# FFT, MLP and soft mixture of experts in one kernel: the float64 conversion's temporaries move to PSUM, w_out @ phi is summed the other way round, the tail's loads wait for the last split, and the order of all instructions is made anew

## The chip, the cores and the metric

One NeuronCore of a Trainium2 chip runs the whole program. The metric is the device time of one execution in microseconds (us), lower is better. The time before is the median of three runs. Engines are named as the profile names them: PE (TensorE, matrix products), PEld (its weight loads), DVE (VectorE), ACT (ScalarE), POOL (GpSimd) and SP (SyncE, which only issues DMAs here).

## What is computed

Three stages run one after the other on 8 sequences of 3072 rows and 256 columns: the real part of a two-dimensional DFT, an MLP whose activation is h - tanh(h), and a soft mixture of 8 experts with 4 slots each.

```python
X = np.fft.fft(np.fft.fft(x, axis=1), axis=2).real.astype(np.float32)   # x: 8 x 3072 x 256
x = X.reshape(8 * 3072, 256)
h = x @ w_in                                # w_in: 256 x 2048
x = ((h - np.tanh(h)) @ w_out).astype(np.float32)
logits = x @ phi                            # phi: 256 x 32
d = softmax of logits over all 24576 rows   # dispatch
slot_out[e] = np.maximum((d.T @ x)[e] @ w1[e], 0) @ w2[e]
c = softmax of logits over the 32 slots     # combine
out = c @ slot_out
```

`w_in` and `w_out` are float64 in memory and reach the chip as pairs of 32-bit words. The chip has to turn them into float32 itself.

## The kernel before

**Three stages.** The *head* loads `w_in` and `w_out` in 16 units of 128x512 numbers (4 chunks `c`, each with two units of either matrix), converts each to float32, and makes the weights of the main loop from them: `Wh`/`Wl` (`w_in` times a small DFT matrix, as a high and a low part), the transposes `winT` and `woT`, products for the logits (`h_1`), and `wp` = `w_out @ phi`. In the same time the 24-point part of the FFT of the first sequence is done in SBUF by POOL, DVE and ACT (`dft24`, line 327 for the additions and 331 for the scalings). The *main loop* runs over 96 tiles of 128 frequency rows, each with 4 groups `g` of 512 hidden columns. The *tail* computes the experts' MLP for the 32 slots and then mixes and stores 8 sequences.

**The conversion** (`load_w`, lines 770 to 814). A unit arrives in `raw`, low and high words alternating. ACT squares the high word read as float32 (`square`, L784) into `cv`. DVE then does six operations of 128x512: `top` (L787, a TENSOR_SCALAR), `sign` (L790), `small` (L794), `power` (L798, a TENSOR_SCALAR), `low` (L802) and `join` (L805). All inputs and outputs are in SBUF: `raw`, `cv`, and the result in `tr`. `cv` has two buffers, so two units are in work at a time.

**w_out @ phi.** Per chunk, `wo_t` (L832) turns `w_out` into `woT`, `wp_t` (L841) multiplies with `phi` as the stationary operand into 32 rows of 512, ACT copies that into a corner of the second sequence's buffer (`wpT`, L962), and after the last chunk `wp_1` (L929) turns it back with 16 transposes.

**A group of the main loop.** PE makes two products `pp` and `qq` (`wide`, L462). DVE moves `pp` to SBUF with a correction (`evac`, L483) and forms `h` (`plus`, L488), POOL the mirror half (`minus`, L491), ACT takes tanh (`act_h`, L500) and rounds to float16 (`act_t`, L508), DVE forms the rest (`low_t`, L512, "t1" below), SP issues a transposing DMA (`turn_t`, L516, into `tt`), and PE adds the result to the logits (`logits`, L543). Two tiles form a pair `p`: its logits give softmax factors, and `slots` (L650) adds to the slots' sums.

**The order.** Each engine runs its instructions in the order in which the program issues them. That order is made when the program is built: a class `Flow` simulates the engines with a cost per operation, rings of buffers (`"B": 7` are the PSUM banks, `"cv"`, `"t"`, `"tt"` and others) and due times from the table `SCHED`, and always issues the operation that can start first. `+B` in an operation's list of buffers asks that one more bank stays free when it takes its own. One Flow plans the head, one the main loop with the tail's first loads, one the tail.

**The tail's loads.** `early` are ten loads into buffers that the main loop has done with (`wot`, `wlw`, `w128w`); they wait until the last group's products are evacuated. `late` are 16 loads of `w2`, 512 KB each, into slots of `tr`. The first `EARLY` = 2 of them are planned in the main loop's Flow, the others in the tail's, behind three loads of saved logits (`load_l`, `lt`).

Of the kernel before, what the change touches and what calls it, by code (L numbers as in the profile page):

```python
# [9 lines left out]
F32 = mybir.dt.float32  # L10
# [38 lines left out]
    "wide0": -0.16, "wide1": 0.762, "z_dft": -4.233, "ls_sum": 13.766, "soft_m": 15.943, "soft_h": 16.77,
    "soft_l": 17.545, "z_acc": 28.408, "evac": 1.257, "z_high": -3.8, "z_low": -1.921, "z_copy": -1.709,  # L50
    "z_turned": 0.891, "low_t0": 4.415, "low_t1": 4.601, "plus": 2.019, "minus": 2.76, "soft_e": 15.988,
    "ls_keep": 14.024, "act_h0": 2.352, "act_h1": 4.079, "act_t0": 4.217, "act_t1": 4.386, "acc_add": 34.456,
    "soft_x": 13.986,
# [172 lines left out]
def fft_mlp_softmoe_kernel(ctx: ExitStack, tc: tile.TileContext, x, w_in, w_out, phi, w1, w2, cq, fd, cm, ct, out):  # L226
# [536 lines left out]
    def clear(_):
        nv.memset(spec, 0.0)
        nv.memset(zacc, 0.0)
        nv.memset(zts[:, :, 0:1], 1.0)
        nv.memset(spt[:, 0:1], 1.0)
        nv.memset(nm[0], 3.0e38)

    def load_w(dst, src, a, u):  # L770
# [37 lines left out]
        hf.add({"A": ca(512)}, square, [("raw", u)], [("f", u)], take="cv")
        hf.add({"V": 0.34}, top, [("raw", u)], [("v", u)])
        hf.add({"V": 0.6}, sign, [("raw", u)], [("v", u)])  # L810
        hf.add({"V": 0.6}, small, [("f", u)], [("v", u)])
        hf.add({"V": 0.34}, power, [("v", u)], [("f", u)])
        hf.add({"V": 0.6}, low, [("raw", u)], [("f", u)], free="raw")
        hf.add({"V": cv(512), "G": cg_(512)}, join, [("v", u), ("f", u)], [u], free="cv")
# [4 lines left out]

    def psum(key, a=None, n=512, rows=128):  # L820
        t = bank(str(key).replace(" ", ""), "hps", n, rows)
        Y[key] = t if a is None else t.rearrange("p (a b) -> p a b", a=a)
        return Y[key]

    def B(*key):
        return f"B:{key}".replace(" ", "")
# [787 lines left out]
```

## Time and profile before

| what | value |
|---|---|
| median of 3 runs | 1541.09 us (1539.62 to 1548.11) |
| the profiled execution: its own time | 1543.61 us |
| its span, first to last instruction | 1541.8 us |
| mean granted TensorE clock | 0.969 of full speed |
| PE busy | 1422.7 us (92% of the span) |
| DVE busy | 1200.6 us (78%) |
| ACT busy | 1147.2 us (74%) |
| POOL busy | 1022.6 us (66%) |

Busy time is summed over the whole span. Shares over the span mix the three stages, whose limits differ, so a stage is read from its own window. "Idle before, releaser" in a row of the trace says how long the engine stood still before the instructions, and what ended it.

### The profile page before, as it was taken

To read this page: it belongs to the slowest core of one execution; us is meant where nothing else is said; L and a number is where in the kernel's file an instruction comes from. 1 tells how busy PE (TensorE), PEld (TensorE's weight loads), DVE (VectorE), ACT (ScalarE), POOL (GpSimd) and SP (SyncE) were. 2 spreads that over 40 slices of the span, in tenths; PEclk is the share of its full clock that TensorE was granted. 3 is DMA by queue.
4 is the path that set the end of the run, shared out by engine and by line. 5 is a ranking of instruction groups with operands and counts; after the bars stand their busy time and mean duration, and the time that the engine had idled before them with its cause. 6 is when DMAs were issued, how large, how long until landed. Compare 5 with 4: busy or idle time off the path is not lost. (4 is left out here: it accounts for less than half of the span.)

```text
span 1541.8 us, 37758 instructions
## 1 busy us (share of the span) xinstructions
PE 1422.7 (92%) x14604; PEld 1053.2 (68%) x14604; DVE 1200.6 (78%) x2046; ACT 1147.2 (74%) x2527; POOL 1022.6 (66%) x760
## 2 busy tenths in 40 slices
PE   2769999999999999999999999999999999996786
PEld 1337777777677777777677777777777767764464
DVE  8998788878788888878787888888787778774462
ACT  2337887878788878888788788887888777773386
POOL 3965589867886897579857986788678922321320
PEclk9789999999999999999999999999999999997899
DMA  6328999989999999999989999999999999889978
GB/s 192 122 74 180 196 198 196 179 152 192 179 180 162 201 183 193 170 191 196 185 150 194 186 190 164 187 201 189 166 182 185 194 178 191 153 169 240 306 291 363
DMA packets 856867, 292.87 MB, mean 190 GB/s; under 512 B 803440, under 2 KB 847344, under 8 KB 854896
## 3 DMA queue, kind: packets, MB, share of 16 engines
q1 hardware_dynamic: 856688, 290.47, 95.4%
q8 instruction: 114, 1.87, 0.5%
q14 instruction: 65, 0.53, 0.1%
HBM read 58.15 MB, written 30.67 MB: 58 GB/s over the span
## 5 line engine op out<-in xcount | busy, mean ns | idle before, releaser
L491 POOL TENSOR_TENSOR h<-pb,h 128x512 f32<-128x512 f32 x288 | 369.1, 1286 | 302.5 <-DVE h L488 270.5
L512 DVE SCALAR_TENSOR_TENSOR tr<-th,tr 128x512 f16<-128x512 f32 x576 | 387.9, 685 | 38.8 <-ACT tr L508 36.5
L500 ACT ACTIVATE th<-h 128x512 f32<-128x512 f32 x576 | 339.9, 602 | 72.8 <-DVE h L488 36.8
L462 PE MATMUL pp<-Wh,zh 128*128 128x512 f32 x960 | 377.2, 410 | 0.2
L462 PE MATMUL qq<-Wh,zh 128*128 128x512 f32 x768 | 333.0, 434 | 5.4 <-DVE pb L483 3.3
L508 ACT ACTIVATE tr<-th 128x512 f16<-128x512 f32 x576 | 332.5, 596 | 7.2 <-ACT qq L497 2.1
L483 DVE SCALAR_TENSOR_TENSOR pb<-W,zts,pp 128x512 f32<-128x512 f32 x288 | 214.7, 746 | 109.1 <-PE pp L462 92.6
L543 PEld LDWEIGHTS <-tt 128*128 128x128 f16 x6144 | 194.9, 96 | 77.5 <-issue 42.6
L543 PE MATMUL L<-WPn,tt 128*128 128x64 f16 (+1 forms) x6144 | 226.2, 185 | 23.3 <-DMA tt<-tr 22.9
L488 DVE SCALAR_TENSOR_TENSOR h<-pb,qq 128x512 f32<-128x512 f32 x288 | 196.2, 684 | 50.4 <-PE qq L462 42.6
L462 PEld LDWEIGHTS pp<-Wh,zh 128*128 128x128 f32 x960 | 182.0, 190 | 44.2 <-issue 1.6
L462 PE MATMUL pp<-Wl,zh 128*128 128x512 f32 x480 | 190.8, 397 | 0.0
L462 PEld LDWEIGHTS qq<-Wh,zh 128*128 128x128 f32 x768 | 146.7, 191 | 51.1 <-DVE tr L512 9.9
L327 POOL TENSOR_TENSOR xb<-xb 128x508 f32<-128x508 f32 (+3 forms) x98 | 150.5, 1541 | 22.0 <-DMA xb<-in_x 14.1
L462 PE MATMUL qq<-Wl,zh 128*128 128x512 f32 x384 | 152.1, 396 | 0.0
L650 PE MATMUL ta<-tr,dh 128*32 128x512 f16 x2304 | 145.6, 389 | 0.0
L327 POOL TENSOR_TENSOR tA<-xb 128x1024 f32<-128x1024 f32 (+2 forms) x69 | 107.0, 1559 | 23.7 <-ACT xb L331 20.7
L462 PEld LDWEIGHTS pp<-Wl,zh 128*128 128x128 f32 x480 | 91.3, 190 | 15.1
L650 PEld LDWEIGHTS <-dh 128*32 128x32 f16 x2304 | 56.1, 98 | 61.2 <-issue 12.5
L327 POOL TENSOR_TENSOR xb<-xb,tA 128x512 f32<-128x512 f32 (+1 forms) x46 | 78.2, 1699 | 19.6 <-DVE xb L327 16.1
L327 POOL TENSOR_TENSOR xb<-tA 128x508 f32<-128x508 f32 (+2 forms) x78 | 84.9, 1095 | 1.6 <-DVE tA L327 1.2
L454 ACT COPY zts<-tps 128x256 f32<-128x256 f32 x96 | 35.7, 372 | 67.3 <-PE tps L450 66.7
(263 smaller groups left out, 2485.1 us busy)
## 6 DMA issues: line engine op xcount, KB each, us to landing
out<-xb SPq DMA_DIRECT2D x14, 1536.0 KB, 5.4
xb<-in_x SPq DMA_DIRECT2D x32, 512.0 KB, 5.0
tr<-in_moe_w SPq DMA_DIRECT2D x16, 512.0 KB, 9.1
tt<-tr SPq DMA_TRANSPOSE x385, 4.8
xb<-in_moe_w SPq DMA_DIRECT2D x12, 512.0 KB, 4.3
raw<-in_moe_w_in SPq DMA_DIRECT2D x8, 512.0 KB, 3.7
xb<-in_x SPq DMA_DIRECT2D x16, 256.0 KB, 3.9
...
```

The lines of the kernel that those rows point to most:

```text
L327: fn = lambda e: e.tensor_tensor(out=out[1](), in0=a[1](), in1=c[1](), op=op)
L454: ns.copy(out=zs[i][3][:, 1:257], in_=zpp.pop(i).rearrange("p a b -> p (a b)"))
L462: nt.matmul(o, z, v, start=first and n == 0, stop=last and n == 2)
L483: nv.scalar_tensor_tensor(out=pb, in0=W128[:, c - (c > FOLD), :], scalar=zs[i][3][:, 129:130], in1=pqs.pop((g, 0)), op0=ALU.mult, op1=ALU.add)
L488: nv.scalar_tensor_tensor(out=hs[g][:, 0, :], in0=pbs[g], scalar=0.5, in1=pqs.pop((g, 1)), op0=ALU.mult, op1=ALU.add)
L491: ng.tensor_tensor(out=hs[g][:, 1, :], in0=pbs.pop(g), in1=hs[g][:, 0, :], op=ALU.subtract)
L500: ns.activation(out=o, in_=hs[g][:, k, :], func=AF.Tanh)
L508: ns.activation(out=place_t(g)[:, 0, k], in_=ths[g, k], func=AF.Copy, scale=T14)
L512: nv.scalar_tensor_tensor(out=t[:, 1, k], in0=ths.pop((g, k)), scalar=T14, in1=t[:, 0, k], op0=ALU.mult, op1=ALU.subtract)
L543: nt.matmul(L[:, pm].rearrange("p b s -> p (b s)")[:, 0:n], tt[:, hl, pm, f, :], WPn[:, 4 * c + f].rearrange("p b s -> p (b s)")[:, 0:n], ...
L650: nt.matmul(tas[p][32 * c:32 * c + 32, :], dhl[p][:, dl, 2 * k + pm, :], ts[c][:, tl, pm, :], start=(k == 0 and n == 0), stop=(i == tiles( ...
```

## The change

Five parts: (1) in the conversion `f` (the old `cv`) and the first intermediate of `top` lie in PSUM banks instead of SBUF; `join` can no longer be placed on POOL, and two `cv` entries only count units in work. (2) `w_out @ phi` uses `woT` as the stationary operand, 8 products of 128x32 a chunk, and lands in the layout that is wanted, so the 16 transposes and the stay in the second sequence's buffer go. (3) The ten early loads wait for the last `low_t` ("t1" of the last group), and `EARLY` is 8. [...] (5) `SCHED` has new values, so the order is another everywhere.

```diff
 SCHED = {
-    "soft_t": 14.447, "logits": 6.467, "slots": 17.843, "soft_d": 16.242, "z_slots": 18.545, "z_turn": -0.459,
+    "soft_t": 14.651, "logits": 6.337, "slots": 17.971, "soft_d": 16.201, "z_slots": 18.711, "z_turn": -1.458,
...
-EARLY = 2
+EARLY = 8
...
         def square(_):
-            Y["f", u] = hp.tile([128, 512], F32, tag="h", name="cv")
+            Y["f", u] = psum(("f", u))
...
         def top(_):
-            nv.tensor_scalar(out=v, in0=tt_[u][:, :, 1], scalar1=3, scalar2=0x3FFFFFF8, op0=ALU.logical_shift_left, op1=ALU.bitwise_and)
+            nv.tensor_scalar(out=psum(("v", u)).bitcast(U32), in0=tt_[u][:, :, 1], scalar1=3, scalar2=0x3FFFFFF8,
+                             op0=ALU.logical_shift_left, op1=ALU.bitwise_and)
 
         def sign(_):
-            nv.scalar_tensor_tensor(out=v, in0=tt_[u][:, :, 1], scalar=0xC0000000, in1=v, op0=ALU.bitwise_and, op1=ALU.bitwise_or)
+            nv.scalar_tensor_tensor(out=v, in0=tt_[u][:, :, 1], scalar=0xC0000000, in1=Y.pop(("v", u)).bitcast(U32),
+                                    op0=ALU.bitwise_and, op1=ALU.bitwise_or)
...
-    def wp_t(c):
-        o = psum(("wp", c), rows=32)
-        for k in range(2):
-            nt.matmul(o, phs[:, k, :], Y.pop(("woT", c, k)), start=(k == 0), stop=(k == 1))
+    def wp_d(c):
+        o = psum(("wp", c), 4, 4 * NS)
+        for f in range(4):
+            for k in range(2):
+                nt.matmul(o[:, f, :], Y["woT", c, k][:, 128 * f:128 * f + 128], phs[:, k, :], start=(k == 0), stop=(k == 1))
+
+    def wp_c(c):
+        ns.copy(out=wp[:, 4 * c:4 * c + 4, :], in_=Y.pop(("wp", c)))
...
-    def wp_1(_):
-        o = Y["wpp"] = bank("wpp", "wpp").rearrange("p (a s) -> p a s", s=NS)
-        for f in range(16):
-            nt.transpose(o[:, f, :], wpT[:, 128 * f:128 * f + 128], eye[0:32, 0:32])
...
-        return [("cq", n)] + x_keys(i), [("zp", i)], f"z B:zp{i}" + f" B:sp{i}" * (n == 0), ""
+        return [("cq", n)] + x_keys(i), [("zp", i)], f"+B zh z B:zp{i}" + f" B:sp{i}" * (n == 0), ""
...
     for n, (fn, a) in enumerate(early):
-        put(4 * NT + 3 + n // 2, {"D": 1.46}, lambda _, fn=fn, a=a: fn(*a), [("pb", last), ("pq", last, 0), ("pq", last, 1)] + [("w", fn)] * (n not in (0, 4, 8)),
+        put(4 * NT + 5 + n // 2, {"D": 1.46}, lambda _, fn=fn, a=a: fn(*a), [("pb", last), ("pq", last, 0), ("pq", last, 1), ("t1", last, 0), ("t1", last, 1)] + [("w", fn)] * (n not in (0, 4, 8)),
```

What this does to the order is shown at two places.

**DVE in the middle of the head**, two units in work. Operations are named by line; `raw_...` is a unit's words as loaded, `tr_83` the result, `cv_...` the SBUF temporary. Before:

```order
L790 SCALAR_TENSOR_TENSOR tr_83<-raw_197,tr_83 128x512
L787 TENSOR_SCALAR tr_83<-raw_205 128x512
L794 SCALAR_TENSOR_TENSOR tr_83<-cv_237,tr_83 128x512
L790 SCALAR_TENSOR_TENSOR tr_83<-raw_205,tr_83 128x512
L798 TENSOR_SCALAR cv_237<-tr_83 128x512
L787 TENSOR_SCALAR tr_83<-raw_233 128x512
L802 SCALAR_TENSOR_TENSOR cv_237<-raw_197,cv_237 128x512
L794 SCALAR_TENSOR_TENSOR tr_83<-cv_285,tr_83 128x512
L805 TENSOR_TENSOR tr_83<-tr_83,cv_237 128x512
```

Now, where `hps_...` is a PSUM bank:

```order
L796 SCALAR_TENSOR_TENSOR tr_83<-raw_193,hps_254 128x512
L812 TENSOR_TENSOR tr_83<-tr_83,hps_209 128x512
L801 SCALAR_TENSOR_TENSOR tr_83<-hps_256,tr_83 128x512
L792 TENSOR_SCALAR hps_275<-raw_203 128x512
L805 TENSOR_SCALAR hps_256<-tr_83 128x512
L796 SCALAR_TENSOR_TENSOR tr_83<-raw_203,hps_275 128x512
L809 SCALAR_TENSOR_TENSOR hps_256<-raw_193,hps_256 128x512
L801 SCALAR_TENSOR_TENSOR tr_83<-hps_273,tr_83 128x512
L812 TENSOR_TENSOR tr_83<-tr_83,hps_256 128x512
```

The number of operations is the same and two units still alternate. Where an operation of two tensors read both from SBUF, it now reads one from SBUF and one from PSUM.

**SP at the end of the main loop**, which issues one DMA after the other. `tt` is a transpose of the main loop, `wot`, `wlw` and `w128w` are early loads, `lsd1<-lsw` saves logits of a pair and `lsd1<-sls` those of the Nyquist row, `tr<-in_moe2_w2` loads `w2`, `lt` loads saved logits. Before:

```order
L516 DMA_TRANSPOSE tt_21884<-tr_83 128x16x128
L1083 DMA wot_21939<-wod_60 128x1024
L516 DMA_TRANSPOSE tt_21957<-tr_83 128x16x128
L516 DMA_TRANSPOSE tt_22009<-tr_83 128x16x128
L516 DMA_TRANSPOSE tt_22037<-tr_83 128x16x128
L1083 DMA wot_21939<-wod_60 128x1024
L516 DMA_TRANSPOSE tt_22077<-tr_83 128x16x128
L1083 DMA wot_21939<-wod_60 128x1024 x2
L1072 DMA wlw_22115<-in_moe2_w1 128x1024
L562 DMA lsd1_58<-lsw_22113 128x128
...
L1075 DMA tr_83<-in_moe2_w2 128x4x256 x2
L1447 DMA lt0_22250<-lsd0_57 128x768
```

Now:

```order
L516 DMA_TRANSPOSE tt_22076<-tr_83 128x16x128
L516 DMA_TRANSPOSE tt_22096<-tr_83 128x16x128
L1080 DMA wot_22114<-wod_60 128x1024
L1069 DMA wlw_22116<-in_moe2_w1 128x1024
L1091 DMA w128w_22136<-in_ct 128x608
L1080 DMA wot_22114<-wod_60 128x1024 x3
L1069 DMA wlw_22116<-in_moe2_w1 128x1024
L562 DMA lsd1_58<-lsw_22134 128x128
L1069 DMA wlw_22116<-in_moe2_w1 128x1024 x2
...
L1072 DMA tr_83<-in_moe2_w2 128x4x256 x8
L1440 DMA lt0_22278<-lsd0_57 128x768
```

Two early loads stood between the last four transposes; now all transposes are issued first. Eight `w2` loads instead of two stand ahead of the first `lt`.

## Rows read from the trace of the kernel before

**Rows 1.** Busy time by stretch: us, then PE, PEld, DVE, ACT, POOL, PEclk, DMA, GB/s.

```profile
60.00:80.00 20.00, 13.65 (x28) 5.82 (x28) 20.00 (x20) 4.22 (x10) 16.62 (x11) 0.72 0.19 55
...
114.40:1404.70 1290.30, 1261.48 (x13727) 953.24 (x13726) 1035.68 (x1808) 1038.97 (x2308) 920.44 (x697) 0.99 1.02 182
```

**Rows 2.** Groups by line, head (0 to 114 us): count, busy us, mean ns, idle before.

```profile
L802 DVE SCALAR_TENSOR_TENSOR cv<-raw,cv 128x512 f32<-128x512 uint32 x16 | 19.3, 1204 | 0.1
L805 DVE TENSOR_TENSOR tr<-tr,cv 128x512 f32<-128x512 f32 x16 | 16.7, 1046 | 0.1
L790 DVE SCALAR_TENSOR_TENSOR tr<-raw,tr 128x512 uint32<-128x512 uint32 x16 | 16.3, 1018 | 0.0
L794 DVE SCALAR_TENSOR_TENSOR tr<-cv,tr 128x512 f32<-128x512 f32 x16 | 15.7, 982 | 0.1
L798 DVE TENSOR_SCALAR cv<-tr 128x512 uint32<-128x512 uint32 x16 | 14.0, 873 | 0.0
L787 DVE TENSOR_SCALAR tr<-raw 128x512 uint32<-128x512 uint32 x16 | 13.1, 818 | 4.4 <-DMA raw<-in_moe_w_in 4.4
...
L859 DVE SCALAR_TENSOR_TENSOR Wl<-hps,Wh 128x512 fp32r<-128x512 f32 x8 | 5.4, 681 | 1.3 <-ACT Wh L854 1.3
```

**Rows 3.** DVE in order of time, head: start us, us, engine, line, tensors.

```profile
17.48 1.74 DVE L327 TENSOR_TENSOR xb<-xb 128x508 f32<-128x508 f32 x1
...
38.26 0.42 DVE L787 TENSOR_SCALAR tr<-raw 128x512 uint32<-128x512 uint32 x1
...
54.89 0.68 DVE L859 SCALAR_TENSOR_TENSOR Wl<-hps,Wh 128x512 fp32r<-128x512 f32 x1
55.49 1.15 DVE L805 TENSOR_TENSOR tr<-tr,cv 128x512 f32<-128x512 f32 x1
...
109.96 0.69 DVE L805 TENSOR_TENSOR tr<-tr,cv 128x512 f32<-128x512 f32 x1
```

**Rows 4.** POOL in order of time, head.

```profile
14.56 1.31 POOL L327 TENSOR_TENSOR xb<-xb 128x508 f32<-128x508 f32 x1 [14.12 <-DMA xb<-in_x]
...
38.84 10.46 POOL L327 TENSOR_TENSOR xb<-xb 128x508 f32<-128x508 f32 x1 [4.13 <-ACT xb L331]
...
54.38 1.71 POOL L327 TENSOR_TENSOR xb<-tB 128x508 f32<-128x508 f32 x1
...
100.52 0.90 POOL L327 TENSOR_TENSOR xb<-tA 128x256 f32<-128x256 f32 x1
```

**Rows 5.** Groups by line, POOL, main loop (114 to 1404 us).

```profile
L327 POOL TENSOR_TENSOR tA<-xb 128x1024 f32<-128x1024 f32 x28 | 66.9, 2388 | 22.8 <-ACT xb L331 20.7 <-DMA tt<-tr 2.1
...
L327 POOL TENSOR_TENSOR xb<-xb 128x508 f32<-128x508 f32 x28 | 35.7, 1274 | 0.0
```

**Rows 6.** Groups by line, PE in the head (0 to 114 us).

```profile
L849 PE MATMUL hps<-tr 128*128 128x512 f32 x20 | 15.5, 903 | 33.9 <-DVE tr L805 22.3 <-DMA tr<-in_fd 11.6
```

**Rows 7.** PE in order of time: the first product of the main loop.

```profile
114.41 0.48 PE L462 MATMUL pp<-Wh,zh 128*128 128x512 f32 x1
```

**Rows 8.** SP's queue in order of time, end of the main loop.

```profile
1400.57 9.10 SPq L516 DMA_TRANSPOSE tt<-tr  x3
1409.73 1.06 SPq L1083 DMA_DIRECT2D wot<-wod  x1
1410.95 3.98 SPq L516 DMA_TRANSPOSE tt<-tr  x1
```

**Rows 9.** DVE there: the last split.

```profile
1404.47 0.69 DVE L512 SCALAR_TENSOR_TENSOR tr<-th,tr 128x512 f16<-128x512 f32 x1
```

**Rows 10.** PE there and in the tail.

```profile
1416.97 0.82 PE L543 MATMUL L<-WPn,tt 128*128 128x64 f16 x16 [3.94 <-DMA tt<-tr]
...
1455.63 3.66 PE L1419 MATMUL sop<-tr,hT 128*32 128x256 f32 x64
```

**Rows 11.** The tile tt from 1385 to 1420 us: its DMAs' time to landing.

```profile
DMA to landing us min/median/max: 4.3/4.5/7.5
```

**Rows 12.** Busy time by stretch, tail; columns as in Rows 1.

```profile
1428.00:1457.00 29.00, 23.76 (x242) 12.35 (x246) 12.61 (x25) 12.21 (x23) 10.68 (x8) 0.88 1.08 358
```

More of the change, by code (lines that the diff above doesn't have):

```diff
@@ L47 @@
 SCHED = {
-    "soft_t": 14.447, "logits": 6.467, "slots": 17.843, "soft_d": 16.242, "z_slots": 18.545, "z_turn": -0.459,
[L49 to L53, printed above, removed]
+    "soft_t": 14.651, "logits": 6.337, "slots": 17.971, "soft_d": 16.201, "z_slots": 18.711, "z_turn": -1.458,
+    "wide0": -0.165, "wide1": 0.725, "z_dft": -5.304, "ls_sum": 13.614, "soft_m": 15.558, "soft_h": 17.152,
+    "soft_l": 17.462, "z_acc": 25.423, "evac": 1.54, "z_high": -2.259, "z_low": -1.816, "z_copy": -1.578,
+    "z_turned": 1.314, "low_t0": 4.303, "low_t1": 5.258, "plus": 1.66, "minus": 2.729, "soft_e": 16.122,
+    "ls_keep": 15.142, "act_h0": 2.255, "act_h1": 3.898, "act_t0": 3.417, "act_t1": 3.987, "acc_add": 28.127,
+    "soft_x": 14.416,
 }
 TB = 16
-EARLY = 2
+EARLY = 8
 HLATE = 0.0
@@ L768, in clear, with psum, B @@
         nv.memset(nm[0], 3.0e38)
+    def psum(key, a=None, n=512, rows=128):
+        t = bank(str(key).replace(" ", ""), "hps", n, rows)
+        Y[key] = t if a is None else t.rearrange("p (a b) -> p a b", a=a)
+        return Y[key]
+    def B(*key):
+        return f"B:{key}".replace(" ", "")
     def load_w(dst, src, a, u):
@@ L802, in low, with join @@
             nv.scalar_tensor_tensor(out=f, in0=tt_.pop(u)[:, :, 0], scalar=2.0 ** -52, in1=f, op0=ALU.mult, op1=ALU.mult)
-        def join(e):
-            vg[e].tensor_tensor(out=vf, in0=vf, in1=Y.pop(("f", u)), op=ALU.add)
+        def join(_):
+            nv.tensor_tensor(out=vf, in0=vf, in1=Y.pop(("f", u)), op=ALU.add)
         hf.add({"D": 1.46}, get, w=[("raw", u)], take="raw", lat=2.0)
[L808 to L814, printed above, removed]
+        hf.add({"A": 0.68}, square, [("raw", u)], [("f", u)], take="cv " + B("f", u))
+        hf.add({"V": 0.6}, top, [("raw", u)], [("v", u)], take=B("v", u))
+        hf.add({"V": 0.7}, sign, [("raw", u)], [("v", u)], free=B("v", u))
+        hf.add({"V": 0.7}, small, [("f", u)], [("v", u)])
+        hf.add({"V": 0.6}, power, [("v", u)], [("f", u)])
+        hf.add({"V": 0.7}, low, [("raw", u)], [("f", u)], free="raw")
+        hf.add({"V": 0.7}, join, [("v", u), ("f", u)], [u], free="cv " + B("f", u))
     tt_ = {}
@@ L818, in fft_mlp_softmoe_kernel @@
     wir = w_in.rearrange("(k p) f -> p k f", p=128)
[L820 to L826, printed above, removed]
     def wo_t(c, k):
@@ L1129, in fft_mlp_softmoe_kernel @@
     for n, (kind, k, fn, r, w) in enumerate(rest):
-        cost = {"A": 0.08 + 0.23 * k} if kind == "A" else {"V": 0.06 + 0.266 * k, "G": 0.17 + 0.53 * k}
-        put(-5 + 10 * n / len(rest), cost, lambda e, fn=fn: fn(vg.get(e)), r, w)
+        cost = {"A": 0.08 + 0.23 * k} if kind == "A" else {"V": 0.15 + 0.267 * k, "G": 0.19 + 0.55 * k}
+        put(-5 + 10 * n / len(rest), cost, lambda e, fn=fn: fn(vg.get(e)), r, w, port="V" if kind == "P" else "")
     for b in range(1, NB):
@@ L1178, in fft_mlp_softmoe_kernel @@
         b_ = (pb_, qb_)[k]
-        stage(sub(act_h), n4, 1, {"A": 0.6}, lambda g: ([("pq", g, k) if whole(g) else ("h", g, k)], [("th", g, k)], "" if whole(g) else "+B " + b_(g),
+        stage(sub(act_h), n4, 1, {"A": 0.6}, lambda g: ([("pq", g, k) if whole(g) else ("h", g, k)], [("th", g, k)], "" if whole(g) else b_(g),
                                                         "wv"[k] if whole(g) else "h" * k), f"act_h{k}")
@@ L1208, in fft_mlp_softmoe_kernel @@
     stage(soft_l, NP, 8, {"V": 0.2}, lambda p: ([("dp", p), ("dh", p)], [("dl", p)], "", f"B:dp{p}"))
-    stage(z_slots, NP, 8, {"T": 0.29}, lambda p: ([("dh", p)] + [("zt", i) for i in tiles(p)], [("zl", p)], f"B:zl{p}", "dd" + " zt" * len(tiles(p))))
+    stage(z_slots, NP, 8, {"T": 0.4}, lambda p: ([("dh", p)] + [("zt", i) for i in tiles(p)], [("zl", p)], f"B:zl{p}", "dd" + " zt" * len(tiles(p))))
     stage(z_acc, NP, 8, {"V": 0.27}, lambda p: ([("zl", p), ("e", p), ("dp", p)], ["zacc"], "", f"B:zl{p}"))
@@ L1246, in fft_mlp_softmoe_kernel @@
     put(8 * NP, {"D": 0.5}, lambda e: s_keep(NB - 1, NB), ["sls", ("lk", NP - 1)], (), "", "", 2.0, "ls_keep")
-    wpk = [("x", 1, k) for k in range(8)]
-    wpk += [("wpT", c) for c in range(4)]
-    put(-30, {"T": 0.6}, lambda e: wp_1(e), wpk, ["wpq"], "B:wpp")
-    put(-30, {"A": 0.53}, lambda e: ns.copy(out=wp, in_=Y.pop("wpp")), ["wpq"], ["wp"], "", "B:wpp")
-    put(-30, {"V": 0.6}, lambda e: top_1(e), ["wp"], ["am0"])
+    put(-30, {"V": 0.6}, lambda e: top_1(e), [("wp", c) for c in range(4)], ["am0"])
     put(-30, {"T": 0.1}, lambda e: top_2(e), ["am0"], ["am1"], "B:am2")
```

39 lines of the change are left out of this document (17 added, 22 removed).

## The prediction

> **What bounds the kernel now.** I read the busy time by stretch first, because the shares over the whole span hide three stages. From 114.4 us to 1404.7 us PE is busy for 1261.5 of 1290.3 us [rows 1]: the main loop is PE's, and the order can win back at most its 28.8 us of idle time, 0.3 us for each of some 95 tiles. In the head it is the other way round: from 60 to 80 us DVE is busy for all 20 us and PE for 13.7 [rows 1], and the groups by line say that PE's first products of a unit wait for DVE's last conversion step, 22.3 us in all [rows 6]. So the head ends when DVE has converted the last unit, at 110.65 us [rows 3], and the main loop's first product follows at 114.41 [rows 7]. Whatever DVE saves before that moves the whole PE-bound loop forward, one for one, until another chain of the head takes over. The third stage is read in order of time: after the last split on DVE at 1405.16 [rows 9] PE waits for transposes until the last logits at 1416.97 [rows 10], with almost nothing else to do.
>
> **The conversion.** Its 96 DVE operations are busy for 19.3 + 16.7 + 16.3 + 15.7 + 14.0 + 13.1 = 95.1 us [rows 2]. Undisturbed, the same operations take 0.42 us (TENSOR_SCALAR) and 0.69 us (two tensors) [rows 3]; their means of 0.82 to 1.20 us are that, plus blocking. The reader is to see whom it hits: at 54.89, with POOL in an addition from 54.38 to 56.09 [rows 4], the operation L859, one input in PSUM and one in SBUF, takes its 0.68 us and the next starts 0.60 us after it; that next one, with both inputs in SBUF, takes 1.15 [rows 3]. All eight L859 together have a mean of 0.681 [rows 2]. POOL is hit as well: an addition that costs 1.27 us in the main loop [rows 5] took 10.46 us here [rows 4].
>
> After the change each of the 96 is like L859: at most one input in SBUF. No row shows a TENSOR_SCALAR that writes to PSUM. Its bounds are 0.42 us (the undisturbed row) and 0.69 (the other operations); I take the upper, since its nearest row by memory is L859. An operation occupies DVE for 0.60 us where the next does not need its result (as at 54.89), and up to 0.69 where it does; the new order alternates two units, so I take 0.63, or 60.5 us for 96. Before, consecutive operations also overlap by 0.08 us (0.68 busy, 0.60 to the next start), so 95.1 us busy is 95.1 - 96 x 0.08 = 87.4 us of DVE's time. **Saved: 87.4 - 60.5 = 26.9 us.** Bounds: 0.60 each for 64 and 0.42 for 32 gives 51.8, saved 35.6; 0.69 for all gives 66.2, saved 21.2.
>
> One FFT addition of 1.74 us [rows 3] leaves DVE for POOL: saved 1.7. Against that, the eight L859 wait for PE and ACT to make their inputs. Before, that cost 1.3 us once [rows 2], because DVE was late for everything. A faster DVE comes earlier: between 0 and 8 x 1.3 = 10.4 us, and I take 3, as the order puts three to five other operations between a unit's last step and the first L859. ACT's squares into PSUM and its copies are covered: ACT was busy for 4.2 of the 20 us [rows 1]. So the head gains 26.9 + 1.7 - 3 = **25.6, say 26 us**, and the last unit is converted at about 85 us.
>
> Is POOL ready by then? It has 47 additions in the head: 10 of 1024 columns at 2.4 us and 11 of 508 at 1.27 [rows 5]; the 10 of 512 I set at 1.3 and the 16 of 256 at half of that, 0.7 (estimates by size from these two rows). That is 24 + 14 + 13 + 11 = 62 us. It starts 14.6 us in, when its data lands, and waits at least 4 us for ACT [rows 4], so it ends near 81 to 87 us instead of 101.4. It is level with DVE, no longer far ahead: this is the first rival.
>
> [...] The row says that an operation reading PSUM costs DVE no more than one that reads SBUF alone: 0.68 against 0.69 us [rows 3]. [...]
>
> **w_out @ phi.** A chunk's 2 products of 32x512 become 8 of 128x32, and 16 transposes, a copy and a stay in a buffer go. All of it is in PE's and ACT's waiting time of the head, or 1 to 2 us of PE at the border to the main loop. I count nothing; if the head becomes PE-bound, it is a gain of that size.
>
> **The tail.** The last transpose starts at 1410.95, because SP first issues three transposes in 9.10 us (3.0 each) and a load in 1.06 [rows 8]. The load is no longer between them, nor in the DMA engines beside them, and a transpose there lands 4.5 us after its start in the median but up to 7.5 [rows 11]. The last could start as soon as its split is done, at 1405.2, and land at 1409.7: 7 us earlier than 1416.97. If SP needs 3.0 us for each of four in a row from 1400.2, the last starts at 1409.2 and lands at 1413.7: 3 us earlier. I take **4 us**. The ten loads behind them start some 10 us later than now. Do they then hold up the tail? They, 16 of w2 and 3 of saved logits are about 14.3 MB (24 loads of 512 KB, 3 of 384 KB and 0.6 MB of constants); at 358 GB/s [rows 12] that is 40 us, so the last w2 lands near 1450. The product that needs it runs at 1455.63 [rows 10] and would come at 1451.6 now: covered by a hair. What SP moves past each other matters here: eight w2 loads pass the saved logits, 4.2 MB or 12 us of DMA, while DVE and POOL need those only for the mixing that follows.
>
> **The main loop's order.** Per tile PE does the same work. Its 28.8 us of idle time [rows 1] may shrink or grow; from the rows I can't tell, so I count 0, with 14 us (half of it) either way in the bounds.
>
> **The sum.** The profiled execution took 1543.6 us, and 1543.6 - 26 - 4 = 1513.6. It lies 2.5 us above the median of 1541.1, so in terms of the median: **1511 us**. With the bounds of the conversion and of L859, and 0 to 7 for the tail, this case reaches from 1498 to 1528.
>
> **The rivals.**
> 1. *Another chain takes over the head.* POOL, ACT's copies in program order and PE at a granted clock of 0.72 [rows 1] are all close behind. If POOL, which ended at 101.4, only loses the 9 us that its one starved addition lost, the main loop starts some 10 us earlier and not 26: 1541 - 10 - 4 = 1527. For it: POOL waited 4.1 us for ACT just there [rows 4]. Against it: POOL's blocking goes too.
> 2. *The tail gives nothing*: the loads that now start later are the bound, since DMA is full after 1417 at 358 GB/s [rows 12]. Then 1515, or 1518 if w2 lands 3 us late.
> 3. *The main loop's order is better*: half of the idle time goes, 1497.
> 4. *Slower.* The spare bank. `z_dft`, `z_turn` and `wide0` must now leave one bank free, so PE's products queue behind ACT's tanh for a bank, tile after tile. It decides above (30 + 7.7) / 95 = 0.4 us of new idle time a tile, more than the 0.3 it has now; at 0.6 us the kernel takes 1511 + 57 = 1568. Against it: PE at 98% leaves no sign of a shortage of banks.
> 5. *The change doesn't do what it says*: POOL blocks operations with one SBUF input too, so DVE keeps its price. Then only the 4 us of the tail remain, 1537. L859 speaks against it.
>
> **How the numbers follow.** About 0.5% (7.7 us) is what a measurement of this kernel can tell from no change. Chances: forecast 0.56, rival 1 0.16, rival 2 0.09, rival 3 0.09, rival 4 0.05, rival 5 0.05. Below 1533.4 lie the forecast and rivals 1 to 3, less a little for two of them going wrong together: faster 0.87. Rival 5 and that little: same 0.08. Rival 4: slower 0.05. The range of 1495 to 1530 leaves out rivals 4 and 5 and the ends of the others.
>
> **What would show it.** The six conversion groups in the head at means of 0.65 to 0.72 us and 62 to 66 us busy in all (a TENSOR_SCALAR at 0.42 would be the lower bound); the last conversion step near 85 us and the first main-loop product near 89; no POOL addition of 10 us; PE idle for 25 to 35 us in the main loop; the last logits 4 us sooner after the last split, and no wait for w2 in the tail. The prediction is wrong if the first product comes after 100 us, if the idle time in the main loop exceeds 60 us, or if the products with w2 wait for DMAs.

## The result and the profile after

The changed kernel takes 1500.97 us (median of 4 runs, 1498.37 to 1502.74) against 1541.07 us for the kernel before: a ratio of 0.973, 95% interval 0.9696 to 0.9763. That is 40 us faster, where 30 were forecast; it lies within the range. The profiled executions (1543.6 and 1499.9 us) differ by 43.7 us. I divide them at two points that every kernel of this study has, the first product of the main loop and the end of the last split on DVE:

| | before | after | difference | forecast |
|---|---|---|---|---|
| first main-loop product | 114.41 | 81.76 | -32.7 | -26 |
| from there to the last split (the loop) | 1290.8 | 1273.6 | -17.2 | 0 |
| last split to the end of the span | 136.6 | 142.8 | +6.2 | -4 |

So in the profiled runs the sum came out 14 us better than forecast, and no line of it was met: two terms gained more, and the third has the other sign.

**The head.** Groups by line on DVE, 0 to 81 us, after; they answer to [rows 2].

```profile
L809 DVE SCALAR_TENSOR_TENSOR hps<-raw,hps 128x512 f32<-128x512 uint32 x16 | 11.0, 687 | 0.0
L805 DVE TENSOR_SCALAR hps<-tr 128x512 uint32<-128x512 uint32 x16 | 11.0, 686 | 0.1
L792 DVE TENSOR_SCALAR hps<-raw 128x512 uint32<-128x512 uint32 x16 | 11.0, 685 | 5.2 <-DMA raw<-in_moe_w_in 4.8 <-ACT W L857 0.3
L801 DVE SCALAR_TENSOR_TENSOR tr<-hps,tr 128x512 f32<-128x512 f32 x16 | 10.9, 684 | 0.1
L812 DVE TENSOR_TENSOR tr<-tr,hps 128x512 f32<-128x512 f32 x16 | 10.9, 680 | 0.1
L796 DVE SCALAR_TENSOR_TENSOR tr<-raw,hps 128x512 uint32<-128x512 uint32 x16 | 10.9, 679 | 0.0
L862 DVE SCALAR_TENSOR_TENSOR Wl<-hps,Wh 128x512 fp32r<-128x512 f32 x8 | 5.5, 682 | 1.2 <-ACT Wh L857 1.2
```

All six steps cost the same now, 65.7 us busy in all instead of 95.1, and L862 (L859 before) waits 1.2 us in all, no more than before. The end of it on DVE in order of time, after:

```profile
74.26 0.68 DVE L812 TENSOR_TENSOR tr<-tr,hps 128x512 f32<-128x512 f32 x1
74.85 0.69 DVE L801 SCALAR_TENSOR_TENSOR tr<-hps,tr 128x512 f32<-128x512 f32 x1
75.45 0.68 DVE L862 SCALAR_TENSOR_TENSOR Wl<-hps,Wh 128x512 fp32r<-128x512 f32 x1
76.05 0.69 DVE L805 TENSOR_SCALAR hps<-tr 128x512 uint32<-128x512 uint32 x1
76.64 0.42 DVE L445 TENSOR_TENSOR zh<-zps,zh 128x256 fp32r<-128x256 f32 x1
76.97 0.69 DVE L809 SCALAR_TENSOR_TENSOR hps<-raw,hps 128x512 f32<-128x512 uint32 x1
77.70 0.69 DVE L812 TENSOR_TENSOR tr<-tr,hps 128x512 f32<-128x512 f32 x1
```

From start to start it is 0.59 to 0.60 us, and 0.73 where a step needs the result of the one just before it (L809 at 76.97, then L812). The last unit is converted at 78.39 instead of 110.65 [rows 3]. POOL is undisturbed beside them too, at 2.37 us an addition of 1024 columns as in the main loop of before (2.39 in the mean [rows 5]); two of its rows in the head, after, one addition behind the other:

```profile
41.98 2.37 POOL L327 TENSOR_TENSOR tA<-xb 128x1024 f32<-128x1024 f32 x1
44.44 2.37 POOL L327 TENSOR_TENSOR xb<-xb 128x1024 f32<-128x1024 f32 x1
```

**The loop.** Busy time of the whole stretch, after (columns as in [rows 1]), then what PE waited for most in it (us, times, longest), after and before:

```profile
81.76:1355.37 1273.61, 1254.51 (x13697) 936.36 (x13701) 1041.22 (x1806) 1025.73 (x2306) 922.07 (x697) 1.00 1.03 185
```

```profile
PE L L543 <- DMA tt<-tr: 8.1, 9, 2.1
```

```profile
PE L L543 <- DMA tt<-tr: 13.4, 19, 1.4
```

In this pair of profiles PE's idle time fell from 28.8 to 19.1 us, its busy time from 1261.9 to 1254.5. The largest wait, that of the logits' products for the DMA transposes of the splits, fell by 5 us.

**The tail**, after, in order of time on PE; then SP's queue, DVE and ACT beside it:

```profile
1363.45 0.82 PE L543 MATMUL L<-WPn,tt 128*128 128x64 f16 x16 [0.89 <-DMA tt<-tr]
...
1395.56 1.12 PE L1406 MATMUL hTp<-w128w,h 128*128 128x128 f32 x4 [7.51 <-ACT h L1454]
1396.61 4.83 PE L1412 MATMUL sop<-tr,hT 128*32 128x256 f32 x64
...
1418.30 4.18 PE L1532 MATMUL op<-R,ct 128*128 128x512 f32 x9 [4.90 <-DVE ct L1430]
```

```profile
1374.23 7.82 SPq L1072 DMA_DIRECT2D tr<-in_moe_w  x8
1382.10 3.40 SPq L1440 DMA_DIRECT2D lt<-lsd  x3
```

```profile
1391.40 2.87 DVE L1467 TENSOR_REDUCE mx<-lt 128x24 f32<-128x768 f32 x3 [7.63 <-DMA lt<-lsd]
```

```profile
1394.09 0.93 ACT L1474 ACTIVATE lt<-lt,desc 128x768 f32<-128x768 f32 x1 [7.67 <-POOL lt L1471]
1394.93 0.58 ACT L1454 ACTIVATE h<-h1p 128x512 f32<-128x512 f32 x1
```

The last logits start 8.1 us after the last split (1355.37) instead of 11.8 [rows 9, 10]: the 3.7 us that the forecast wanted. But the saved logits `lt` are now issued behind eight loads of `w2`. Their maximum on DVE waits 7.63 us for them, and their exponential on ACT stands ahead of the second half of `h` in ACT's order, so `hTp`, `sop` and, in the end, the first product of the mixing come late.

### The profile page after: what moved, and what is told of

Its sections match the earlier page's. It is cut to its first block, busy times and chain, and to the rows that moved or that the text cites. A ratio compares the mean times of both kernels' runs of the same rounds, so it can differ in the third digit from the quotient of the medians.

```text
span 1498.2 us, 38001 instructions
## 1 busy us (share of the span) xinstructions
PE 1405.2 (94%) x14636; PEld 1037.0 (69%) x14636; DVE 1172.2 (78%) x2039; ACT 1132.7 (76%) x2527; POOL 1009.0 (67%) x766
## 4 chain that ended last, share of the span: by engine, by line
PE 84%; DMA 6%; DVE 5%; issue 2%; ACT 1%; SPq 1%; POOL 0%; DVEq 0%; ACTq 0%; POOLq 0%
PE qq L462 22%; PE pp L462 22%; PE L L543 11%; PE ta L650 9%; DMA tt<-tr 4%; PE op L1532 3%; PE L L536 2%; PE tps L450 1%; PE zps L411 1%; PE LT L580 1%; PE zlp L634 1%; PE zps L414 1%; PE zps L412 1%; PE zps L413 1%; PE L L537 1%
## 5 line engine op out<-in xcount | busy, mean ns | idle before, releaser
L512 DVE SCALAR_TENSOR_TENSOR tr<-th,tr 128x512 f16<-128x512 f32 x576 | 382.4, 683 | 39.9 <-ACT tr L508 39.5
L462 PE MATMUL pp<-Wh,zh 128*128 128x512 f32 x960 | 374.7, 407 | 1.7 <-DVE tr L512 1.2
L462 PE MATMUL qq<-Wh,zh 128*128 128x512 f32 x768 | 328.9, 428 | 4.8 <-DVE tr L512 4.8
L462 PEld LDWEIGHTS pp<-Wh,zh 128*128 128x128 f32 x960 | 180.7, 188 | 46.2 <-DVE tr L512 5.3
L462 PE MATMUL pp<-Wl,zh 128*128 128x512 f32 x480 | 190.5, 397 | 0.0
L462 PEld LDWEIGHTS qq<-Wh,zh 128*128 128x128 f32 x768 | 145.0, 189 | 32.7 <-DVE tr L512 5.7
L327 POOL TENSOR_TENSOR xb<-xb 128x508 f32<-128x508 f32 (+3 forms) x103 | 146.1, 1420 | 29.4 <-DMA xb<-in_x 14.5
L462 PE MATMUL qq<-Wl,zh 128*128 128x512 f32 x384 | 151.3, 394 | 0.0
L650 PE MATMUL ta<-tr,dh 128*32 128x512 f16 x2304 | 142.6, 383 | 0.0
L441 ACT CAST zh<-zps 128x256 fp32r<-128x256 f32 x96 | 35.8, 373 | 100.5 <-PE zps L414 88.5
L462 PEld LDWEIGHTS pp<-Wl,zh 128*128 128x128 f32 x480 | 90.9, 189 | 14.8
L462 PE MATMUL qq<-Wm,zh 128*128 128x512 f32 x288 | 83.3, 398 | 0.0
```

The lines of the kernel that those rows point to most:

```text
L327: fn = lambda e: e.tensor_tensor(out=out[1](), in0=a[1](), in1=c[1](), op=op)
L441: ns.copy(out=z[1], in_=zpp[i])
L462: nt.matmul(o, z, v, start=first and n == 0, stop=last and n == 2)
L512: nv.scalar_tensor_tensor(out=t[:, 1, k], in0=ths.pop((g, k)), scalar=T14, in1=t[:, 0, k], op0=ALU.mult, op1=ALU.subtract)
L650: nt.matmul(tas[p][32 * c:32 * c + 32, :], dhl[p][:, dl, 2 * k + pm, :], ts[c][:, tl, pm, :], start=(k == 0 and n == 0), stop=(i == tiles( ...
```

## The experiments

"Loop" and "split to end" are the stretches of the table above, in us, from the one profiled run of each kernel, which for e5, e7, e9 and e12 was also its slowest, 3 to 8 us above its median. Ratios are to the kernel before as timed beside each run, with their 95% intervals. "My theory" and the lettered rivals are those of the text recorded before each run.

| run | ratio | first product | loop | split to end |
|---|---|---|---|---|
| change as made | 0.973 (0.9696-0.9763) | 81.8 | 1273.6 | 142.8 |
| e1_head_alone | 0.9882 (0.9859-0.9906) | 84.9 | 1301.5 | 136.3 |
| e2_order_alone | 0.9935 (0.9911-0.996) | 112.1 | 1280.3 | 137.0 |
| e3_tail_alone | 1.0036 (1.0022-1.0051) | 113.4 | 1290.0 | 142.2 |
| e4_early2 | 0.9677 (0.9654-0.9701) | 81.8 | 1274.8 | 135.0 |
| e5_lt0_first | 0.9658 (0.9642-0.9673) | 81.9 | 1274.4 | 137.1 |
| e6_old_table | 0.9708 (0.9694-0.9723) | 84.1 | 1269.2 | 143.2 |
| e7_old_rules | 1.0195 (1.0166-1.0225) | 84.3 | 1348.8 | 145.4 |
| e8_old_tail | 0.9712 (0.9692-0.9732) | 82.6 | 1273.3 | 140.9 |
| e9_old_costs | 1.0087 (1.0062-1.0111) | 82.6 | 1336.5 | 142.5 |
| e10_old_spares | 0.986 (0.9841-0.9879) | 84.6 | 1297.0 | 142.7 |
| e11_old_table_early2 | 0.9656 (0.9638-0.9674) | 82.2 | 1273.9 | 135.7 |
| e12_old_phi | 0.9693 (0.9675-0.9712) | 82.9 | 1273.9 | 144.2 |

### One part at a time, on the kernel before

**e1_head_alone**: `f` and `v` of `load_w` in PSUM, with the costs of these seven operations in the planner's head and `join` on DVE alone; the rest as before.

```diff
-            Y["f", u] = hp.tile([128, 512], F32, tag="h", name="cv")
+            Y["f", u] = psum(("f", u))
-            nv.tensor_scalar(out=v, in0=tt_[u][:, :, 1], ...)
+            nv.tensor_scalar(out=psum(("v", u)).bitcast(U32), in0=tt_[u][:, :, 1], ...)
```

> The kernel before with the conversion's two temporaries in PSUM and nothing else. My theory (the head's gain is the shorter conversion alone, and it carries undiminished to the end): conversion operations at 0.69 us as in the changed kernel, last one ended near 80, first main-loop product at 82 to 86 (before 114.41), main loop still 1288 to 1292 long, time 1508 to 1513, that is 29 to 33 us faster. Rival A (the shorter main loop also comes from the head, since the loop begins under other conditions): 1490 to 1497. Rival B (the conversion is quick only with the order made anew, POOL's additions stretching it otherwise): first product after 95, time 1520 or more.

Measured: 1524.82 us, the kernel before beside it 1543.2. The head did what my theory said: the six groups have means of 681 to 690 ns, and the first product comes at 84.91, 29.5 us sooner. Only 18 us of that are left at the end. The loop is 10.7 us longer than before, and the rows say by what; its busy time, and its largest wait:

```profile
84.91:1386.41 1301.50, 1261.90 (x13729) 953.89 (x13728) 1033.27 (x1810) 1038.34 (x2307) 917.89 (x695) 1.00 1.00 181
```

```profile
PE L L543 <- DMA tt<-tr: 26.3, 31, 2.1
```

PE works as long as before (1261.9) but waits 26.3 us for transposes instead of 13.4. The planner lays the main loop's order behind the head's, and with another head it made another order: in the traces, PE's instructions in the loop come in another order, line by line, than before. (e3 below keeps the order of before, and its loop is 1290.0 us.) "It carries undiminished to the end" is refuted, and so is rival A. Rival B fails on its mechanism, the conversion being quick beside POOL's additions with the old order too, although the time it gave (1520 or more) is met for another reason.

**e2_order_alone**: `SCHED`, the planner's costs for the main loop and the rules on spare banks as in the change, with one new entry of the table `LATES` (`acc_add`), and nothing else. With the costs goes a rule that FFT operations which either DVE or POOL can take are no longer planned on DVE at the same time as others on POOL; by the rules on spare banks `z_dft`, `z_turn` and `wide0` ask for the bank kept free (`+B`) where `act_h` asked before.

> The kernel before with the change's table of order, its costs and its rules on spare banks in the main loop, and nothing else. My theory (the order made anew shortens the main loop by itself): head unchanged, first product at 114 to 115, from there to the last split 1272 to 1278 instead of 1290.8, TensorE idle in it about 19 us instead of 28.8, time 1523 to 1528. Rival A (order moves nothing, as I predicted): 1538 to 1544. Rival B (the new rules on spare banks cost, and the gain comes from elsewhere): above 1545.

Measured: 1532.0 us, 10 less. The loop is 10.5 us shorter, a little less than expected (time and loop lie outside my theory's ranges by 4 and 2 us), and the wait for transposes is 4.3 us. So the order made anew is a gain by itself, and rival A, my own forecast of 0, falls. The head's end also moved, by 2.3 us.

**e3_tail_alone**: the wait for the last split and `EARLY`.

```diff
-EARLY = 2
+EARLY = 8
-        put(4 * NT + 3 + n // 2, {"D": 1.46}, ..., [("pb", last), ("pq", last, 0), ("pq", last, 1)] + ...
+        put(4 * NT + 5 + n // 2, {"D": 1.46}, ..., [("pb", last), ("pq", last, 0), ("pq", last, 1), ("t1", last, 0), ("t1", last, 1)] + ...
```

> The kernel before with the ten early tail loads behind the last split and eight instead of two w2 loads ahead of the saved logits, and nothing else. My theory (4 us won at the last logits, then given back because the saved logits land later and the second half of h waits behind their exponential on ScalarE): last split to last logits 8 instead of 11.8 us, a wait of 5 to 8 us at the second h transpose, time 1538 to 1545, no net gain. Rival A (the wait at h comes from the order made anew elsewhere and not from the eight w2 loads): no such wait, time 1534 to 1538. Rival B (loads started later delay the whole tail, DMA being busy throughout): 1546 or more.

Measured: 1547.8 us, a loss of 0.36%. Last split to the end of the logits is 8.7 us instead of 12.6, and the wait at the second `h` transpose is there (PE's waits from 1404 to 1470 us):

```profile
PE hTp L1413 <- ACT h L1461: 5.5, 1, 5.5
PE L L543 <- DMA tt<-tr: 5.4, 4, 1.9
PE op L1539 <- DVE ct L1437: 5.4, 1, 5.4
```

So the wait belongs to `EARLY = 8` and not to the order of the loop. By price, though, it is worse than my theory said (no net gain): 0.36% is 5.5 us. The time of 1547.8 is one that rival B gave, the loads that start later; e4 and e8 below part these two edits, on the changed kernel.

The three ratios alone add up to -1.18 - 0.65 + 0.36 = -1.47%; together the parts give -2.7%. Of the missing 19 us, 17 lie in the loop: +10.7 (e1) and -10.5 (e2) make nothing, and the change has -17.2.

### The tail

**e4_early2** (changed kernel) and **e5_lt0_first** (e4 with the first block of saved logits ahead of six `w2` loads, the other two behind).

```diff
-EARLY = 8
+EARLY = 2
```

> The changed kernel with two instead of eight w2 loads ahead of the saved logits, as before. My theory (the eight w2 loads hold up the saved logits, and these the mixing, whose first product waited 4.9 us for its transposed factors): the saved logits land 6 to 8 us sooner, the wait of 7.5 us at the second h transpose goes, the first mixing product comes 3 to 6 us sooner (1418.30 in the changed kernel), time 1495 to 1498 against 1501. Rival A (DMA is busy without a gap from 1362 to 1406, so the w2 loads put behind simply become the wait in their turn): 1499.5 to 1502.5. Rival B (the late w2 loads cost more than the late logits): 1503 or more.

Measured: 1493.12 us, 8 less than the changed kernel, 2 us better than my theory's best. On PE, then DVE, e4:

```profile
1391.20 1.44 PE L1406 MATMUL hTp<-w128w,h 128*128 128x128 f32 x8
1392.58 3.66 PE L1412 MATMUL sop<-tr,hT 128*32 128x256 f32 x64
```

```profile
1387.49 2.66 DVE L1467 TENSOR_REDUCE mx<-lt 128x24 f32<-128x768 f32 x3
```

Counted from the last split (1356.61 here), the maximum comes after 30.9 us instead of 36.0, `sop` after 36.0 instead of 41.2, and the mixing's first product (1411.28) after 54.7 instead of 62.9. No product waits for a `w2` load, although 14 of them are now behind the logits. Rival A falls.

> The changed kernel with two w2 loads ahead as in e4_early2, and of the three first loads of saved logits only the first ahead of the next six w2 loads. My theory (the tail's pace is set by the first block of saved logits and by the first eight w2 loads, both wanted by 1392; the second and third block can come later): 1 to 3 us faster than e4_early2, 1490 to 1492. Rival A (the w2 chain alone sets the end there, DMA being full, and two blocks of logits are too little traffic to matter): 1492.5 to 1494.5. Rival B (the later blocks hold up ScalarE's row, as in the changed kernel): 1496 or more.

Measured: 1490.46 us, with a ratio whose interval overlaps that of e4; its own profiled run (1495.27, its slowest) has a slower tail (137.1 against 135.0 us) and the second `sop` at 1407.30 instead of 1404.36. The time alone lies in my theory's range, but two such runs don't tell it from rival A; rival B falls.

**e8_old_tail**: e4 without the wait for the last split.

```diff
-            ..., [("pb", last), ("pq", last, 0), ("pq", last, 1), ("t1", last, 0), ("t1", last, 1)] + ...
+            ..., [("pb", last), ("pq", last, 0), ("pq", last, 1)] + ...
```

> The changed kernel with the tail as it was: two w2 loads ahead, and the ten early loads not behind the last split. Beside e4_early2 this prices the wait for the last split alone. My theory: last split to last logits 12 instead of 8.9 us, and the end 2 to 4 us later than e4_early2, 1495 to 1497. Rival A (what the logits lose is won back by weights that come sooner): 1492 to 1494. Rival B (it is the loads' earlier start that counts, since DMA is full from there on): 1488 to 1491.

Measured: 1498.89 us, and 5.9 us more from split to end than e4. The last two groups of logits on PE, e8:

```profile
1365.93 0.82 PE L543 MATMUL L<-WPn,tt 128*128 128x64 f16 x16 [5.40 <-DMA tt<-tr]
1370.33 0.82 PE L543 MATMUL L<-WPn,tt 128*128 128x64 f16 x16 [3.58 <-DMA tt<-tr]
```

The last starts 14.4 us after the last split, that of e4 8.3 us after it, and the 6 us are kept to the end of the span. By the ratios it is 5 us, with intervals that overlap a little. So beside e8 the wait for the last split pays, and rivals A and B fall. Beside the kernel before it pays less, since with the new order of the loop the old tail itself is worse: its last logits start 11.8 us after the split in before and 14.4 in e8, and from split to end it is 136.6 and 140.9 us. In e4 the first product of the mixing comes 2.7 us sooner after the split than in before, and of the end 1.6 us are left (135.0 against 136.6). `EARLY = 8` costs 8.

### What in the order shortens the loop

**e6_old_table** (changed kernel, the old numbers of `SCHED`) and **e7_old_rules** (new numbers; old costs and old rules on spare banks).

```diff
-    "soft_t": 14.651, "logits": 6.337, ...
+    "soft_t": 14.447, "logits": 6.467, ...
```

> The changed kernel with the old table of numbers that sets the main loop's order, its new costs and rules kept. My theory (the main loop's gain is the order by which the DMA transposes stay ahead of TensorE, and this is in the table): main loop 1285 to 1302 instead of 1273.6, the wait of the logits' products for transposed tiles 13 to 27 us instead of 8.1, time 1511 to 1528. Rival A (the gain lies in the costs and the rules on spare banks): loop 1271 to 1278, time 1498 to 1504. Rival B (half and half): 1505 to 1510.

> The changed kernel with the old costs and rules on spare banks in the main loop, the new table kept. My theory (the table carries it): loop within 6 us of 1273.6, time 1498 to 1506. Rival A (the rules carry it): loop 1285 to 1302, time 1511 to 1528. A third outcome, that table and rules fit only each other, shows as a loss of over 10 us in this run and in e6_old_table alike.

Measured: 1498.03 and 1572.13 us. My theory that the table carries the gain falls twice: without the new table the loop is 1269.2 us, as good or better; with it, on the old costs and rules, it is 1348.8. (The third outcome, that table and rules fit only each other, falls with e6, which loses nothing.) So I split costs from rules, on the old table, where e1 (both old, loop 1301.5) and e6 (both new, 1269.2) are the corners.

**e9_old_costs** and **e10_old_spares**.

```diff
-    stage(lambda g: wide(g, 0), ..., kind({"T": 0.77}, {"T": 1.54}), ...
+    stage(lambda g: wide(g, 0), ..., kind({"T": 0.7}, {"T": 1.39}), ...
-    stage(slots, NT, 4, {"T": 1.5}, k_slots)
+    stage(slots, NT, 4, {"T": 1.65}, k_slots)
```

```diff
-        return [("cq", n)] + x_keys(i), [("zp", i)], f"+B zh z B:zp{i}" + ...
+        return [("cq", n)] + x_keys(i), [("zp", i)], f"z B:zp{i}" + ...
-        ..., "" if whole(g) else b_(g), ...
+        ..., "" if whole(g) else "+B " + b_(g), ...
```

> As e6_old_table (changed kernel, old table, main loop 1269.2), with the old costs in the main loop's plan too; the new rules on spare banks stay. e1_head_alone has old costs, old rules and old table behind the quick head, and its loop is 1301.5. My theory now (the rules on spare banks carry the gain: a tanh row no longer waits in the plan for a spare bank, so the transposes are issued sooner before the products that read them): loop 1266 to 1276, wait for transposed tiles 8 to 17 us, time 1495 to 1504. Rival A (the costs carry it): loop 1290 to 1305, wait 20 us or more, 1518 to 1532. Rival B (the order is a matter of luck from plan to plan, any edit moving the loop by 10 us and more): a loop outside both, or under 1262.

> As e6_old_table, with the old rules on spare banks; the new costs stay. My theory (rules carry it): loop 1290 to 1305, wait for transposed tiles 20 us or more, time 1518 to 1532. Rival A (costs carry it): loop 1266 to 1276, time 1495 to 1504. Rival B (luck from plan to plan): this and e9_old_costs both lose over 10 us, or neither does.

Measured: 1558.33 and 1523.66 us. e10 by itself came out as my theory had it in loop and time (without the new rules the gain is gone; the wait for transposes is 17.5 us, less than its 20), but e9 refutes it: with the new rules and the old costs the loop is longer than any corner. Loops, on the old table:

| | old rules | new rules |
|---|---|---|
| old costs | 1301.5 (e1) | 1336.5 (e9) |
| new costs | 1297.0 (e10) | 1269.2 (e6) |

The new rules cost 35 us with the old costs and save 28 with the new ones. (The corners are not quite clean. e1 also has the old tail and the old sum of `w_out @ phi`, which leave the loop at 1273 to 1274 in e8 and e12, and the old costs of the rest of the head's plan, which no run tries alone. e10 lacks the new entry of `LATES`, which e9 keeps.) Neither half carries the gain, as rival B said (both lose over 10 us): rules and costs count only as the plan that they make together. What a bad plan looks like is seen in e9, PE in order of time:

```profile
295.87 0.60 PE L543 MATMUL L<-WPn,tt 128*128 128x64 f16 x16 [0.93 <-DMA tt<-tr]
298.43 0.82 PE L543 MATMUL L<-WPn,tt 128*128 128x64 f16 x16 [1.96 <-DMA tt<-tr]
...
302.08 0.82 PE L543 MATMUL L<-WPn,tt 128*128 128x64 f16 x16 [0.36 <-DMA tt<-tr]
304.09 0.82 PE L543 MATMUL L<-WPn,tt 128*128 128x64 f16 x16 [1.18 <-DMA tt<-tr]
```

and the same stretch by engine (PE, PEld, DVE, ACT, POOL, clock, DMA share, GB/s):

```profile
296.00:300.00 4.00, 1.66 (x34) 1.43 (x33) 0.45 (x1) 1.59 (x4) 3.92 (x3) 0.71 1.02 199
300.00:304.00 4.00, 2.02 (x27) 1.13 (x26) 0.29 (x1) 2.21 (x7) 3.18 (x3) 0.50 1.00 175
304.00:308.00 4.00, 3.45 (x26) 3.07 (x27) 0.42 (x1) 1.16 (x2) 3.48 (x2) 0.50 0.00 0
```

Here the order has one group of logits after another and no wide product (L462) between them. PE takes each as its transpose lands; DVE and ACT get little that is new to split (DVE is busy for 0.3 to 0.45 of 4 us), and from 304 the DMA engines are idle. The pipeline has run empty and has to fill again, at a granted clock of 0.50. Over the whole loop the wait for transposes is 29.4 us in e9 and 10.9 in e6. Which of the costs makes the difference was not tried.

**e11_old_table_early2**: e6 with `EARLY = 2`.

> As e6_old_table with two w2 loads ahead of the saved logits, as in e4_early2: what the experiments so far point to as the best. My theory (the 8 us that e4_early2 won in the tail and the 3 us of e6_old_table lie in different stretches and add): 1489 to 1492, last split to the end 135 us. Rival (the tail's gain hangs on the order that the table made): 1495 to 1499.

Measured: 1492.5 us, ratio 0.9656. The tail's 8 us are there (135.7); of e6's shorter loop nothing is seen in this profile (1273.9), so the table's 3 to 4 us are not shown. PE's order in the loop is the same in e6 and e11, line by line; the 4.7 us between their loops are what two executions of one order can differ by, and a smaller difference between loops tells nothing. e4, e5 and e11 are all better than the change as made by 0.5 to 0.7%, and among themselves not to be told apart.

**e12_old_phi**: the changed kernel with the old `w_out @ phi` (`wp_t`, `wp_1` and its copies).

> The changed kernel with w_out @ phi summed as before (16 products of 512 columns, four copies out of PSUM, 16 transposes). As the prediction has it, this costs nothing: 1499.5 to 1503, first main-loop product within 1 us of 81.76. Rival (the four long products behind the last converted unit stand in front of the first main-loop product, as 2.99 us of them do in e1_head_alone, and the 16 transposes after it): first product 83 to 85, time 1503 to 1506. The other rival (the plan of the main loop moves with it): a loop outside 1268 to 1279.

Measured: 1499.42 us, first product at 82.87, loop 1273.9. No loss at the end, as forecast; the 1.1 us at the border to the loop lie between the expectation and its rival and are not seen in the time.

## Why the prediction was right and where not

**What bounds the kernel.** The three stages were read rightly, and the head's end followed DVE's last conversion step: 78.39 and 81.76 now, 3.4 us apart, 3.8 before. But the step "whatever DVE saves before that moves the whole PE-bound loop forward, one for one" failed. e1 saved 29.5 us there and kept 18, because the planner answers a new head with a new order of the loop, 10.7 us longer in e1.

**The conversion** was right in its mechanism and mis-sized by 6.7 us: 32.3 at the last step instead of 25.6. I took 0.63 us of DVE's time for an operation, and in the mean it is 0.61; the 96 of before took 88.6 us from start to start and not 87.4. These two make 3.1 us. And I put 3 us on new waits of L859, and there are none (1.2 in all against 1.3 before): another 3.1 us. The upper bound for a TENSOR_SCALAR into PSUM, 0.69, was the right choice: 0.685 and 0.686. POOL's last addition before the loop ended at 77.8, level with DVE as forecast, so rival 1 did not come. Operations that read PSUM take 0.68 to 0.69 us, as much as an operation of two SBUF tensors did undisturbed (0.69 [rows 3]). And POOL and the conversion no longer hold each other up: beside POOL's additions at 41.98 and 44.44, of 2.37 us each, DVE's steps of after take 0.68 to 0.69 and start every 0.59 to 0.61. The trace of before showed this in one place (54.89) and the change made it the rule; rival 5 falls with it. But the prediction read the condition too simply, as the count of SBUF inputs alone. The TENSOR_SCALARs of before had one SBUF input too and were blocked like the others (2.57 us instead of 0.42 [rows 3], beside a POOL addition of 2.67 instead of 2.37), here on DVE, then on POOL:

```profile
32.43 2.57 DVE L798 TENSOR_SCALAR cv<-tr 128x512 uint32<-128x512 uint32 x1
```

```profile
32.03 2.67 POOL L327 TENSOR_TENSOR xb<-xb,tA 128x1024 f32<-128x1024 f32 x1
```

What sets them free in after is that their output lies in PSUM: two of them beside POOL's addition at 44.44 take 0.68 us each (44.61 and 45.21), and in e1, where little but the temporaries moves, both groups have a mean of 0.688. But there they no longer reach their 0.42 us.

**The main loop's order** is the step that failed: "from the rows I can't tell, so I count 0". It is worth 10.5 us alone and 17.2 in the change, and the bound of 14 was too small (the range of the sum, 1498 to 1528, left even that out). The step under it, that "the order can win back at most its 28.8 us of idle time", fails too, since the order moves PE's busy time as well. The loops of e4, which has PE's order of the change, and of e11, whose order is another:

```profile
81.84:1356.61 1274.77, 1259.29 (x13686) 940.06 (x13689) 1040.28 (x1806) 1026.83 (x2306) 922.48 (x697) 0.99 1.03 185
82.19:1356.07 1273.88, 1245.61 (x13690) 945.85 (x13693) 1046.73 (x1806) 1030.86 (x2306) 921.15 (x697) 1.00 1.03 185
```

Both loops are 16 to 17 us shorter than before. In e4 the gain is nearly all idle time (15.5 us are left of 28.8); in e11 the idle time is 28.3 us as before, and the gain is all busy time.

One thing that goes with longer busy time is the clock. In before, PE in order of time, and the stretch behind it:

```profile
405.02 0.40 PE L462 MATMUL qq<-Wh,zh 128*128 128x512 f32 x1
408.45 0.44 PE L450 MATMUL tps<-cms,z 128*128 128x128 f32 x2 [3.02 <-DVE tr L512]
...
410.12 0.63 PE L462 MATMUL qq<-Wh,zh 128*128 128x512 f32 x1
```

```profile
404.00:408.00 4.00, 1.42 (x7) 0.81 (x5) 3.91 (x3) 0.81 (x3) 3.77 (x3) 1.00 1.26 181
408.00:412.00 4.00, 3.34 (x13) 2.48 (x13) 3.46 (x7) 2.62 (x10) 1.61 (x2) 0.64 0.91 182
412.00:416.00 4.00, 4.00 (x29) 3.21 (x30) 2.23 (x5) 1.22 (x5) 2.94 (x4) 0.51 0.79 143
```

After the wait of 3.02 us the granted clock was 0.50 from 409.4 to 415.6 us, and a product of 128x512 took 0.63 us (410.12) instead of 0.40 (405.02, at a clock of 1.00). Over the loop's pieces of 5 us, (1 - clock) x 5 us, summed where the clock was under 0.95, is 10.0 us before and 1.6 after, as much as the busy time fell (7.4). But this does not carry the shorter loop. With PE's order of the change it is 6.6 us in e4 and 3.4 in e5, and their loops and that of e8 are as long (1273 to 1275), with less idle time; with the order of before PE is busy for 3 us less in e3 (1258.9), and the loop is 1290.0. The clock's loss differs between executions of one order by up to 5 us, the length of these four loops by 1.5. What in the order sets that length stays open. Rival 3 gave 1497 for a better order, the closest in time, but by luck: its own term is 14 us of idle time, where idle time fell by 9.7, and the errors in the head (6.7 us) and the tail (10.2) have opposite signs. Rival 4, the spare bank, did not come in the change as made. Its rules are not harmless, though: with the old costs they make the loop 35 us longer than e1's (e9), by waits for transposes above all (29.4 us), where the rival had a queue for a bank.

**The tail.** The 4 us at the last logits were right (3.7 here), but not that they reach the end: without `EARLY = 8`, in e4, 1.6 us of them do. Of the loss of 6.2 us, `EARLY = 8` makes 7.8 (142.8 against 135.0 in e4). The step that failed is "DVE and POOL need those only for the mixing that follows". ACT ran its work in the order that it was given, and the exponential of the saved logits (1394.09) stood ahead of the second half of `h` (1394.93); and the mixing's first product, 8 us later after the last split than in e4, waits for these very logits. "Covered by a hair" was asked of the `w2` loads, which nobody waited for; the loads that had been passed were the late ones. (Of the eight loads that the prediction lets pass, two stood ahead before already; the change moved six.)

**The sum** hid this: in the profiled runs the head gained 6.7 us and the loop 17.2 more than forecast, and the tail lost 10.2 of it. That the time lies within the range is in part luck.
